# The loads of v for the first 256 queries of batch 0 go to ScalarE's queue, and the order of the beginning is ranked anew

## The chip, the core and the metric

The kernel runs on one core of one Trainium2 chip. The metric is the device time of one execution in microseconds (us); a lower time is better. One execution was also recorded by the profiler, and every time below is from that recording or from the list of executions.

## What is computed

Block-causal attention over 8 batches, 8 heads, 576 positions and head size 64 in float32, and on its output a SwiGLU feed-forward layer with 512 model columns and 1536 hidden columns.

```python
scores = scale * np.matmul(q, k.transpose(0, 1, 3, 2))
mask = block_i >= block_j                  # blocks of 64 positions
scores = np.where(mask, scores, -1000000000.0)
scores = scores - np.max(scores, axis=-1, keepdims=True)
attn = np.exp(scores)
attn = attn / (np.sum(attn, axis=-1, keepdims=True) + 1e-09)
x = np.matmul(attn, v)                     # then heads side by side: 4608 rows of 512
g = x @ w_gate
out = (g * sigmoid(g) * (x @ w_val)) @ w_out
```

## The kernel before, in words

The program is a list of tasks, each for one engine: TensorE (PE), VectorE (DVE), ScalarE (ACT), GpSimd (POOL) or SyncE's DMA queue (SP). A task has a rank, a cost, the tasks it waits for and the buffers it takes. A planner in the program (`in_order`) runs through time with these costs: whenever an engine is free, it takes the ready task with the lowest rank whose buffers are free. What comes out is the order in which each engine gets its instructions. On the chip each engine works through its own list in that order and waits where something is not there yet. So a change of ranks changes no computation, only the order on each engine, and which of several like buffers a task gets.

**Attention.** `attention(R, b, h, ...)` makes the tasks of one pair of heads. For batches 0 and 1 the pairs are cut into the first 256 queries (0 to 256) and the rest (256 to 576). `FIRST` holds a rank for each of the four pairs of each part, used for loads and values (R) and, less 0.1, for scores (Q). For 0 to 256 two pairs share one set of buffers, as two lanes. The steps and their lines:
- L411: two loads each for q and k (one per head), into `qk`. Only for the first 256 queries of batch 0 does k go through ScalarE's queue; the rest goes through SP's.
- L435 on PE: turns q and k with `ident`; L443 on ACT copies them to `parts`.
- L461 on PE: scores into PSUM. For the first 256 queries of batch 0 they stay there: L503 hides what may not be seen, L506 copies a first part to `mx`, both on ACT, and L726 and L729 on DVE take the maximum over key chunks. Otherwise L479 copies them to `sc`, L493 hides, L729 takes the maximum.
- L733 on POOL: maximum over the 128 partitions. L757 on DVE: subtracts it. L761 on ACT: Exp.
- L778: the loads of v, ranked `LATER` behind R. L801 on PE: values and, in batch 0, sums by a product with `ones`.
- L828 to L835 on DVE: invert the sums and divide; L355 and L358 split the result in a high and a low part, the x of the feed-forward tile.

**Weights.** `weight(i, kind)` brings blocks of 128 hidden columns of w_gate, w_val and w_out (kinds 0, 1, 2), in this fixed order: L968 loads 512 KB on SP; L983 and L987 on ACT and L992 and L997 on DVE build a float32 from the words; L1002 on ACT and L1005 on DVE make the high and low part. L1024 stores w_out's parts. `PIECES[i]` ranks the steps of block i, `AHEAD` the load alone.

**Feed-forward.** L1124 on PE makes gate and value products, L1223 to L1225 the output products; from tile 12 on another scheme with L1498 and L1619 to L1621. `SIDE` ranks the first two tiles among the attention.

**Later batches.** Rank `10 + b - LEAD`; their scores and maxima stand `EAGER` ahead of that. L672 are their score products.

Where the planner sees a gap for PE before 215 us, `keep_busy` puts in products of `ones` (L1836) whose result nobody reads.

Of the kernel before, what the change touches and what calls it, by code (L numbers as in the profile page):

```python
# [18 lines left out]
def kernel(  # L19
# [17 lines left out]
    nc = tc.nc  # L37
# [3 lines left out]
    P = 128  # L41
# [4 lines left out]
    SP = NKC * P  # L46
# [3 lines left out]
    XT = 256  # L50


    LEAD, EAGER = 1.69311, 0.3

    SUMS = 2
    ALONE = 3
# [4 lines left out]

    FINE = 4

    AHEAD = {(0, 1): 2.01, (0, 2): 2.07, (1, 0): 2.03, (1, 1): 2.5, (1, 2): 2.5}
    LATER = 0.6

    PIECES = [
        (2.46498, 1.85126, 2.0295),
        (4.86232, 5.94853, 3.63137),
        (4.59615, 2.52017, 1.48427),  # L70
        (3.86967, 3.05824, 5.34888),
        (1.93206, 3.59139, 2.41171),
        (5.13877, 6.90631, 5.83015),
        (3.57653, 2.93377, 2.93471),
        (0.0797053, 1.36382, 0.915695),
        (-2.09572, -5.85789, -4.34371),
        (-7.47749, -5.87222, -3.82425),
        (-7.64215, -9.14061, -8.44419),
        (-12.1092, -9.50108, -10.8836),
    ]  # L80

    SIDE = (2.97811, 4.18833)

    PATIENCE = 10.0
    FILL = 0.6

    FIRST = {
        0: [(0, 256, (-4.21445, 2.40818, 2.05548, 2.12375)), (256, 576, (-2.9124, -2.06995, -6.61901, -4.10645))],
        1: [(0, 256, (4.0214, 3.93624, 4.15916, 3.63076)), (256, 576, (-2.93177, 1.89587, 2.55533, 4.50202))],
    }  # L90
    PAIRS = 3
    PLAIN = NT // XT - 2 * PAIRS
# [62 lines left out]
    def add(engine, cost, rank, fn, after=(), bufs=(), port=False, mode=""):  # L155


        t = Task(engine, cost, rank, fn, after, bufs, port, mode)
        for a in after:
            if a is not None:  # L160
                a.next.append(t)
                t.waits += 1
        for u in bufs:
            u.left += 1
        t.n = len(tasks)
        tasks.append(t)
        return t
# [198 lines left out]
    def attention(R, b, h, a, e, early, bufs, lane):  # L366
# [10 lines left out]
        qk, prt, sc, mx, vt, xu, sr = bufs  # L377
# [393 lines left out]

        ps = Buf("at", also=banks)

        def load_v():
            nf = e // P
            for j, hd in enumerate(heads):
                cols = slice(j * D, (j + 1) * D)
                nc.sync.dma_start(  # L778
                    out=vt[0][:, 2 * lane : 2 * lane + nf, cols],
                    in_=v[b, hd, 0 : nf * P].rearrange("(c p) d -> p c d", p=P),  # L780
                )
            if e > nf * P:
# [155 lines left out]
    def weight(i, kind):  # L938
# [154 lines left out]
    def feed_forward(j, t0, w, xs):  # L1093
# [777 lines left out]
```

## Time and profile before

| what | us |
|---|---|
| median of 3 executions (1148.14 to 1149.58) | 1148.32 |
| the profiled execution, its own time | 1151.43 |
| its span, first to last instruction | 1149.7 |
| PE busy in it | 1127.7 |
| DVE, ACT, POOL busy | 888.5, 605.4, 320.9 |

An engine that is busy for 98% of the span leaves some 22 us in which it could be faster without less work; the stretches of the trace show where these lie. PE's busy time holds the products of `ones` too.

### The profile page before, as it was taken

The numbers are of one execution on the slowest core, as the hardware profiler recorded it, in microseconds if no ns is written. First come the engines' busy times: TensorE is split into PE (matmuls) and PEld (weight loads), VectorE is DVE, ScalarE is ACT, GpSimd is POOL, SyncE is SP. The second block draws the span as 40 slices with busy tenths as digits, with TensorE's granted clock in tenths as the row PEclk, the third lists the DMA queues.
The fourth block names the chain that finished last, engine by engine and source line by source line (L and its number), as shares of the span: only waits on it lengthen the run. The fifth ranks groups of instructions, "written<-read, shape, count | busy, mean of one in ns | idle before, by whom it ended". The sixth has DMA issues, their size and how long they took to land.

```text
span 1149.7 us, 22749 instructions
## 1 busy us (share of the span) xinstructions
PE 1127.7 (98%) x8728; PEld 995.9 (87%) x8728; DVE 888.5 (77%) x1526; ACT 605.4 (53%) x1126; POOL 320.9 (28%) x139
## 2 busy tenths in 40 slices
PE   7999999999999999999999999999999999999998
PEld 5677778898899898888888889888999999999997
DVE  5899898687787889989899898888753855656554
ACT  5888777565554555455565555455422433334323
POOL 3213111036643543334434535444320000000000
PEclk9999999999999999999999999999999999999999
DMA  8767757676665767876786758673468867767761
GB/s 196 192 183 186 204 167 267 171 210 182 167 158 147 203 178 206 225 220 173 206 224 186 207 159 246 175 205 119 167 235 259 272 217 235 236 229 247 234 201 69
DMA packets 294445, 228.92 MB, mean 199 GB/s; under 512 B 196608, under 2 KB 245008, under 8 KB 294336
## 3 DMA queue, kind: packets, MB, share of 16 engines
q1 hardware_dynamic: 291760, 226.75, 67.3%
q8 instruction: 68, 1.11, 0.4%
q10 hardware_dynamic: 2576, 0.72, 0.3%
q14 instruction: 41, 0.34, 0.1%
HBM read 190.45 MB, written 36.96 MB: 198 GB/s over the span
## 4 chain that ended last, share of the span: by engine, by line
PE 84%; DMA 5%; DVE 4%; ACT 4%; SPq 1%; issue 1%; POOL 0%; DVEq 0%; POOLq 0%; ACTq 0%
PE gv L1124 31%; PE gv L1498 15%; PE at L801 6%; PE at L672 6%; PE po L1223 5%; PE po L1224 5%; PE po L1225 5%; PE po L1620 1%; PE po L1619 1%; PE at L1621 1%; PE po L1621 1%; PE at L1620 1%; PE at L1619 1%; DMA wo<-in_moe_w_val_dram 1%; DMA wo<-in_moe_w_gate_dram 1%
## 5 line engine op out<-in xcount | busy, mean ns | idle before, releaser
L852 POOL PARTITION_ALL_REDUCE mx<-mx x48 | 180.1, 3799 | 212.0 <-DVE mx L729 153.8
L733 POOL PARTITION_ALL_REDUCE mx<-mx x80 | 138.3, 1778 | 309.6 <-DVE mx L729 218.9
L1124 PE MATMUL gv<-xhl,v_all 128*128 128x256 f32 x1728 | 219.3, 279 | 1.7 <-DVE v_all L1005 1.1
L1124 PEld LDWEIGHTS gv<-xhl,v_all 128*128 128x128 f32 x1728 | 206.5, 188 | 7.4 <-issue 2.8
L757 DVE TENSOR_TENSOR sc<-sc,mx 128x640 f32<-128x640 f32 (+6 forms) x168 | 123.6, 774 | 16.4 <-POOL mx L733 16.4
L761 ACT ACTIVATE sc<-sc 128x1024 f32<-128x1024 f32 (+3 forms) x104 | 106.2, 1032 | 48.0 <-DVE sc L757 47.4
L1124 PE MATMUL gv<-xhl,g_even 128*128 128x256 f32 x864 | 117.9, 281 | 0.0
L1124 PE MATMUL gv<-xhl,g_odd 128*128 128x256 f32 x864 | 116.9, 282 | 0.0
L1124 PEld LDWEIGHTS gv<-xhl,g_even 128*128 128x128 f32 x864 | 110.8, 188 | 6.9 <-issue 1.9
L729 DVE TENSOR_TENSOR mx<-mx,sc 128x128 f32<-128x128 f32 (+2 forms) x180 | 110.9, 619 | 2.1 <-ACT sc L493 0.4
L1124 PEld LDWEIGHTS gv<-xhl,g_odd 128*128 128x128 f32 x864 | 106.2, 188 | 5.1 <-issue 2.6
L1223 PE MATMUL po<-wo,hhl 128*128 128x512 f32 x252 | 101.6, 403 | 0.0
L1224 PE MATMUL po<-wo,hhl 128*128 128x512 f32 x252 | 98.7, 392 | 0.0
L1225 PE MATMUL po<-wo,hhl 128*128 128x512 f32 x252 | 98.3, 390 | 0.0
L801 PE MATMUL at<-sc,v 128*64 128x128 f32 (+4 forms) x848 | 90.0, 361 | 2.2 <-ACT parts L443 1.4
L689 ACT ACTIVATE sc<-at 128x576 f32<-128x576 f32 (+1 forms) x96 | 75.8, 835 | 27.7 <-PE at L672 27.6
L1176 ACT CAST hhl<-t 128x512 fp32r<-128x512 f32 x72 | 44.7, 621 | 82.8 <-DVE t L1171 70.8
L801 PEld LDWEIGHTS at<-sc,v 128*64 128x64 f32 x848 | 56.0, 137 | 35.8 <-ACT parts L443 1.6
L1179 DVE TENSOR_TENSOR hhl<-t,hhl 128x512 fp32r<-128x512 f32 x72 | 71.3, 990 | 17.2 <-ACT hhl L1176 17.2
L729 DVE TENSOR_TENSOR mx<-sc 128x896 f32<-128x896 f32 (+2 forms) x68 | 70.0, 1031 | 7.4 <-ACT sc L701 3.9
L672 PE MATMUL at<-parts,qk 64*128 64x288 f32 (+4 forms) x864 | 73.3, 310 | 0.7 <-ACT sc L689 0.7
L672 PEld LDWEIGHTS at<-parts,qk 64*128 64x128 f32 x864 | 62.0, 185 | 9.6 <-issue 1.1
(223 smaller groups left out, 2041.2 us busy)
## 6 DMA issues: line engine op xcount, KB each, us to landing
wo<-wo_d SPq DMA_DIRECT2D x164, 512.0 KB
v_all<-sum_d SPq DMA_DIRECT2D x36, 512.0 KB
v_all<-sum_d SPq DMA_DIRECT2D x72, 256.0 KB
sum_d<-wo SPq DMA_DIRECT2D x48, 256.0 KB
v<-in_v_dram SPq DMA_DIRECT2D x64, 128.0 KB
qk<-in_q_dram SPq DMA_DIRECT2D x112, 72.0 KB
out_dram<-ob SPq DMA_DIRECT2D x30, 256.0 KB
qk<-in_k_dram SPq DMA_DIRECT2D x104, 72.0 KB
```

Source lines behind the costliest of these rows:

```text
L672: nc.tensor.matmul(ps[0][:, x, o : o + w], lhsT=part(1, kl)[own(x), c * P : (c + 1) * P], rhs=part(0, ql)[own(x), qs : qs + w], start=n == ...
L729: nc.vector.tensor_tensor(into, prev, of(c), op)
L733: nc.gpsimd.partition_all_reduce(m, m, channels=P, reduce_op=bass_isa.ReduceOp.max)
L757: nc.vector.tensor_tensor(piece(c), scores_of(c), m, ALU.subtract)
L761: nc.scalar.activation(x, x, AF.Exp)
L801: nc.tensor.matmul(ps[0][own(x), 1 - i if sums else i, q0 - s0 : s1 - s0], lhsT=ones if sums else vt[0][:, 2 * lane + c, own(x)], rhs=sc[0 ...
L852: nc.gpsimd.partition_all_reduce(m, m, channels=P, reduce_op=bass_isa.ReduceOp.add)
L1124: nc.tensor.matmul(o, lhsT=hilo[a][:, d], rhs=xs[d][1][b][:, 0:w], start=ds[0] == 0 and n == 0, stop=ds[-1] == NDC - 1 and n == len(trio) - 1,
L1223: nc.tensor.matmul(po, lhsT=hi, rhs=whi, start=i + y == 0, stop=False)
L1224: nc.tensor.matmul(po, lhsT=hi, rhs=wlo, start=False, stop=False)
L1225: nc.tensor.matmul(po, lhsT=lo, rhs=whi, start=False, stop=i + y == NFC - 1)
L1498: nc.tensor.matmul(ps[0][:, half * XT : (half + 1) * XT], lhsT=stationary(a, j, s), rhs=part(o, j, m), start=begin and k == 0, stop=all(a ...
```

## The change

The numbers of `LEAD`, `EAGER`, `AHEAD`, `LATER`, `PIECES`, `SIDE` and `FIRST` are others (two rows of them are shown), and the loads of v for the first 256 queries of batch 0 go through ScalarE's queue.

```diff
-    LEAD, EAGER = 1.69311, 0.3
+    LEAD, EAGER = 1.571386, 3.533263
...
-    AHEAD = {(0, 1): 2.01, (0, 2): 2.07, (1, 0): 2.03, (1, 1): 2.5, (1, 2): 2.5}
+    AHEAD = {(0, 1): -0.083496, (0, 2): 1.482327, (1, 0): -5.864524, (1, 1): 2.679334, (1, 2): 8.33569}
...
-        def load_v():
+        other = early and a == b == 0
+
+        def load_v(queue=nc.scalar if other else nc.sync):
             nf = e // P
             for j, hd in enumerate(heads):
                 cols = slice(j * D, (j + 1) * D)
-                nc.sync.dma_start(
+                queue.dma_start(
                     out=vt[0][:, 2 * lane : 2 * lane + nf, cols],
                     in_=v[b, hd, 0 : nf * P].rearrange("(c p) d -> p c d", p=P),
                 )
...
-        vl = dma(R + (LATER if early else 0.0), 512.0 * e, load_v, [], [vt], 3 if e % P else 2, packet=256)
+        vl = dma(R + (LATER if early else 0.0), 512.0 * e, load_v, [], [vt], 3 if e % P else 2, "ACT" if other else "SP", 256)
```

Lines behind L771 move down by two in the changed kernel. Each engine has the same instructions as before but for the eight loads, some products of `ones` (107 instead of 96) and the PSUM buffers. TensorE's last 1866 matmuls stand in the same order; ahead of that much moves.

**SP's first issues.** `qk_0_138` and `qk_0_146` (after: `qk_0_145`) are the two buffers for q and k, `v_0_78` and `v_0_80` the two for v, `wo_0_...` the five for weights. Before:

```order
L411 DMA qk_0_138<-in_q_dram 96x3x64 x2
L778 DMA v_0_78<-in_v_dram 128x2x64 x2
L411 DMA qk_0_146<-in_q_dram 96x3x64 x4
L411 DMA qk_0_138<-in_q_dram 96x3x64 x2
L968 DMA wo_0_108<-in_moe_w_gate_dram 128x4x256
L778 DMA v_0_80<-in_v_dram 128x2x64 x4
L778 DMA v_0_78<-in_v_dram 128x2x64 x2
L411 DMA qk_0_138<-in_q_dram 96x4x64 x2
L411 DMA qk_0_138<-in_k_dram 96x6x64 x2
L968 DMA wo_0_109<-in_moe_w_val_dram 128x4x256
```

After:

```order
L411 DMA qk_0_138<-in_q_dram 96x3x64 x2
L411 DMA qk_0_145<-in_q_dram 96x3x64 x2
L411 DMA qk_0_138<-in_q_dram 96x3x64 x2
L411 DMA qk_0_145<-in_q_dram 96x3x64 x2
L970 DMA wo_0_108<-in_moe_w_gate_dram 128x4x256
L411 DMA qk_0_138<-in_q_dram 96x4x64 x2
L411 DMA qk_0_138<-in_k_dram 96x6x64 x2
L970 DMA wo_0_109<-in_moe_w_val_dram 128x4x256
```

The eight issues of v are gone, and the second lane of `qk_0_138` comes ahead of that of the other buffer.

**ScalarE's start.** Before:

```order
L411 DMA qk_0_138<-in_k_dram 96x3x64 x2
L1664 ACT_TABLE_LOAD
L1664 ACTIVATE seen<-seen 128x1
L411 DMA qk_0_146<-in_k_dram 96x3x64 x4
L411 DMA qk_0_138<-in_k_dram 96x3x64 x2
L443 ACTIVATE parts_0_86<-gv_0_169 128x288
L443 ACTIVATE parts_1_87<-gv_0_175 128x288
L503 ACTIVATE at_0_155<-at_0_155,unseen 128x4x64
L506 COPY mx_0_201<-at_0_155 128x2x128
```

After, from the fourth row on (ahead of it stand two issues each of k for `qk_0_138`, v for `v_0_78` and k for `qk_0_145`):

```order
L411 DMA qk_0_138<-in_k_dram 96x3x64 x2
L1666 ACT_TABLE_LOAD
L1666 ACTIVATE seen<-seen 128x1
L443 ACTIVATE parts_0_86<-gv_0_170 128x288
L443 ACTIVATE parts_1_87<-gv_0_176 128x288
L411 DMA qk_0_145<-in_k_dram 96x3x64 x2
L780 DMA v_0_80<-in_v_dram 128x2x64 x2
L503 ACTIVATE at_0_156<-at_0_156,unseen 128x4x64
L443 ACTIVATE parts_0_86<-gv_0_170 128x288
L443 ACTIVATE parts_1_87<-gv_0_176 128x288
L780 DMA v_0_78<-in_v_dram 128x2x64 x2
L506 COPY mx_0_228<-at_0_156 128x2x128
```

All eight first issues stand ahead of the table load now, and six issues and two copies stand between the first operands (L443) and L506. The last two issues of v follow after four more rows. Further down, the conversion of the first w_gate block (L1002) moved from just ahead of the first step of the first w_val block (L983) to just behind it.

**SP up to the third w_val block** (`wo_0_110`), from the stores of w_out's first parts on. Before (the q and k of `qk_0_138` that stand second after the change stand ahead of these rows):

```order
L1024 DMA wo_d<-g_even_75 128x4x128
L1024 DMA wo_d<-g_even_77 128x4x128
L411 DMA qk_0_146<-in_q_dram 96x3x64 x2
L411 DMA qk_0_146<-in_k_dram 96x3x64 x2
L778 DMA v_0_80<-in_v_dram 128x4x64 x2
L783 DMA v_0_80<-in_v_dram 64x2x64
L411 DMA qk_0_146<-in_q_dram 96x3x64 x2
L411 DMA qk_0_146<-in_k_dram 96x3x64 x2
L968 DMA wo_0_109<-in_moe_w_gate_dram 128x4x256
L411 DMA qk_0_138<-in_q_dram 96x3x64 x2
L968 DMA wo_0_110<-in_moe_w_val_dram 128x4x256
```

After:

```order
L1026 DMA wo_d<-g_even_75 128x4x128
L1026 DMA wo_d<-g_even_77 128x4x128
L411 DMA qk_0_138<-in_q_dram 96x4x64 x2
L411 DMA qk_0_138<-in_k_dram 96x6x64 x2
L411 DMA qk_0_145<-in_q_dram 96x3x64 x2
L411 DMA qk_0_145<-in_k_dram 96x3x64 x2
L780 DMA v_0_80<-in_v_dram 128x4x64 x2
L785 DMA v_0_80<-in_v_dram 64x2x64
L970 DMA wo_0_108<-in_moe_w_gate_dram 128x4x256
L411 DMA qk_0_145<-in_q_dram 96x3x64 x2
L411 DMA qk_0_145<-in_k_dram 96x3x64 x2
L970 DMA wo_0_110<-in_moe_w_val_dram 128x4x256
```

The stores stand first, the third w_gate block stands ahead of the last q and k of `qk_0_145`, and the q pair ahead of w_val is gone from there.

## Rows read from the trace of the kernel before

**Rows 1.** The page: the span and TensorE's busy time.

```profile
span 1149.7 us, 22749 instructions
PE 1127.7 (98%) x8728; PEld 995.9 (87%) x8728; DVE 888.5 (77%) x1526; ACT 605.4 (53%) x1126; POOL 320.9 (28%) x139
```

**Rows 2.** Load by stretch: from and to in us, length, then busy time and instructions of each engine, TensorE's granted clock as a share of full speed, share of the DMA engines, GB/s.

```profile
0.00:41.04 41.04, 32.20 (x323) 26.03 (x324) 27.24 (x69) 27.06 (x53) 14.12 (x20) 0.96 0.77 194
10.00:15.00 5.00, 3.53 (x36) 2.94 (x36) 2.77 (x6) 3.79 (x10) 1.51 (x2) 1.00 0.72 174
15.00:20.00 5.00, 4.44 (x54) 3.91 (x54) 3.33 (x9) 2.07 (x6) 4.20 (x4) 1.00 1.02 239
...
75.00:215.00 140.00, 135.59 (x1005) 110.79 (x1004) 122.93 (x212) 107.21 (x194) 23.37 (x19) 1.00 0.69 201
100.00:120.00 20.00, 19.96 (x158) 16.30 (x155) 17.10 (x30) 15.75 (x32) 5.82 (x4) 1.00 0.93 224
600.00:800.00 200.00, 200.00 (x1600) 177.83 (x1598) 176.88 (x282) 106.74 (x188) 92.75 (x32) 1.00 0.67 190
```

**Rows 3.** TensorE up to 75 us: its longest wait (total, times, longest), and the busy time of L1836 alone in that stretch.

```profile
PE at L461 <- ACT parts L443: 4.1, 3, 3.1
...
0.00:75.00 75.00, 16.48 (x192) 14.05 (x192) 0.98 0.72 184
```

**Rows 4.** SP's queue in order of time: start, length, line, what is issued, how many.

```profile
0.73 0.91 SPq L411 DMA_DIRECT2D qk<-in_q_dram  x2
...
3.17 4.03 SPq L411 DMA_DIRECT2D qk<-in_q_dram  x6
...
7.84 2.99 SPq L778 DMA_DIRECT2D v<-in_v_dram  x6
10.93 1.58 SPq L411 DMA_DIRECT2D qk<-in_q_dram  x2
...
14.61 0.51 SPq L968 DMA_DIRECT2D wo<-in_moe_w_val_dram  x1
...
34.31 0.85 SPq L411 DMA_DIRECT2D qk<-in_q_dram  x2
...
45.08 0.47 SPq L968 DMA_DIRECT2D wo<-in_moe_w_gate_dram  x1
...
46.65 0.47 SPq L968 DMA_DIRECT2D wo<-in_moe_w_val_dram  x1
```

**Rows 5.** ScalarE in order of time (ACTq: its DMA issues; in brackets the idle time before the row and what ended it).

```profile
0.74 0.96 ACTq L411 DMA_DIRECT2D qk<-in_k_dram  x2
1.73 1.28 ACT L1664 ACT_TABLE_LOAD   x1 [1.73 <-PEq L1854]
...
3.47 2.42 ACTq L411 DMA_DIRECT2D qk<-in_k_dram  x4
5.93 0.71 ACT L443 ACTIVATE parts<-gv 128x288 f32<-128x288 f32 x2 [2.71 <-DMA qk<-in_k_dram]
7.67 0.45 ACT L503 ACTIVATE at<-at,unseen 128x256 f32<-128x256 f32 x1 [1.02 <-PE at L461]
8.15 0.37 ACT L506 COPY mx<-at 128x256 f32<-128x256 f32 x1
...
20.40 0.78 ACT L983 ACTIVATE ob<-wo 128x512 f16<-128x512 f32 x1 [3.33 <-DMA wo<-in_moe_w_val_dram]
...
22.52 0.63 ACT L443 ACTIVATE parts<-at 128x576 f32<-128x576 f32 x1
...
52.46 0.79 ACT L983 ACTIVATE ob<-wo 128x512 f16<-128x512 f32 x1 [1.20 <-DMA wo<-in_moe_w_val_dram]
```

**Rows 6.** VectorE's waits up to 41.04 us: total, times, longest.

```profile
DVE sc L757 <- POOL mx L733: 3.5, 2, 2.2
DVE wo L992 <- ACT ob L983: 1.8, 2, 1.3
DVE sr L828 <- PE at L801: 1.2, 1, 1.2
```

**Rows 7.** VectorE in order of time.

```profile
8.55 0.42 DVE L726 COPY mx<-at 128x256 f32<-128x256 f32 x1 [4.17 <-ACT mx L506]
...
41.04 2.93 DVE L757 TENSOR_TENSOR sc<-sc,mx 128x640 f32<-128x640 f32 x5
...
53.44 0.45 DVE L828 STREAM_TRANSPOSE sr<-po 128x256 f32<-128x256 f32 x1 [1.25 <-ACT sr L895]
```

**Rows 8.** TensorE in order of time, between 306 and 318 us: products of 128 rows (L1124) and a block of products of 64 rows (L672).

```profile
306.82 0.51 PE L1124 MATMUL gv<-xhl,g_even 128*128 128x256 f32 x3
307.26 1.07 PE L672 MATMUL at<-parts,qk 64*128 64x288 f32 x12
...
315.96 1.57 PE L1124 MATMUL gv<-xhl,g_even 128*128 128x256 f32 x12
317.37 0.87 PE L1124 MATMUL gv<-xhl,g_odd 128*128 128x256 f32 x6
```

**Rows 9.** The chain that ended last, its first two pieces: start, length, what; a load's length runs from issue to landing.

```profile
0.74 2.71 DMA qk<-in_k_dram
3.47 2.90 DMA qk<-in_k_dram
```

More of the change, by code (lines that the diff above doesn't have):

```diff
@@ L62 @@
     FINE = 4
-    AHEAD = {(0, 1): 2.01, (0, 2): 2.07, (1, 0): 2.03, (1, 1): 2.5, (1, 2): 2.5}
-    LATER = 0.6
+    AHEAD = {(0, 1): -0.083496, (0, 2): 1.482327, (1, 0): -5.864524, (1, 1): 2.679334, (1, 2): 8.33569}
+    LATER = 0.595047
     PIECES = [
[L68 to L79, printed above, removed]
+        (2.46498, 1.85126, 1.989959),
+        (3.078149, 5.94853, 4.5426),
+        (5.243281, -1.760877, -0.59026),
+        (3.314534, 5.058387, 7.706737),
+        (2.073692, 6.770616, 1.885983),
+        (-1.674509, 7.596873, 5.770771),
+        (8.760551, 3.105905, 9.704257),
+        (0.045307, 1.36382, 0.244583),
+        (-1.025389, -0.885477, -4.516175),
+        (-7.289443, -6.137035, -6.344597),
+        (-7.64215, -9.202601, -6.57203),
+        (-20.296957, -11.697245, -12.264919),
     ]
-    SIDE = (2.97811, 4.18833)
+    SIDE = (2.97811, 4.689617)
     PATIENCE = 10.0
@@ L87 @@
     FIRST = {
-        0: [(0, 256, (-4.21445, 2.40818, 2.05548, 2.12375)), (256, 576, (-2.9124, -2.06995, -6.61901, -4.10645))],
-        1: [(0, 256, (4.0214, 3.93624, 4.15916, 3.63076)), (256, 576, (-2.93177, 1.89587, 2.55533, 4.50202))],
+        0: [(0, 256, (-7.882981, 2.009396, 1.545746, 2.12375)), (256, 576, (-3.938665, -3.824963, -14.529285, -4.103347))],
+        1: [(0, 256, (3.274971, 5.869312, 2.105466, 3.587042)), (256, 576, (-2.910293, 1.091971, 2.928513, 8.395196))],
     }
@@ L782, in load_v @@
             if e > nf * P:
-                nc.sync.dma_start(
+                queue.dma_start(
                     out=vt[0][0 : e - nf * P, nf, :].rearrange("p (h d) -> p h d", h=2),
```

## The prediction

> **What bounds the kernel now.** I read the page first, then TensorE's load by stage, its waits, and then the first 55 us engine by engine, since the change works there. The page shows TensorE busy for 1127.7 of 1149.7 us [rows 1]. By stage it is full between 600 and 800 us (200.00 of 200), and between 75 and 215 us it lacks 4.4 of 140 us [rows 2]. So from some 75 us on the time is TensorE's own work, and a change pays only by what TensorE idles, or fills with products of `ones` that nobody reads, before that. Those fillers take 16.48 us, all before 75 us, and the waits come on top: 4.1 us for score operands that ScalarE evicts (3.1 of them in one piece) [rows 3]. Before 75 us TensorE is starved, and the engines to ask are ScalarE, VectorE and the loads.
>
> The long piece of 3.1 us is read on ScalarE: it stood idle 3.33 us until the first w_val block landed, converted it at 20.40, and only behind that, at 22.52, evicted the operands [rows 5]. ScalarE works in order, so an eviction that was ready waited behind a weight. That load was issued at 14.61 [rows 4], 5.8 us before. And SP reached it late: it ran from 0.73 to 10.83 through q and v issues, and took up the next q loads at 10.93 [rows 4].
>
> **Part 1, eight loads of v leave SP's queue.** Six of them took 2.99 us [rows 4], 0.50 each, so SP gains 4.0 us. The whole cannot be had: the next q and k loads overwrite a buffer whose transposes need the loads of the second head pair. These are now SP's third pair instead of its fifth, so they can be issued by about 4 us instead of 7; the last k pair of ScalarE (below: issued by 5.9, landing 2.7 to 2.9 later [rows 9]) then lets the transposes run at some 8.4 to 9.0. I put the next q loads at 9.1 instead of 10.93 and, with the shorter row of issues, w_val at 12.0 instead of 14.61: 2.6 us earlier. Both ends: 10.6 by issue time alone, 14.6 if nothing comes of it. It lands at 17.8 if it takes as long as before.
>
> Against this speaks the load of the DMA engines: their share is 1.02 between 15 and 20 us [rows 2], so a load issued earlier need not land earlier. From 10 to 15 us it was 0.72, so there is room for what moves forward into that stretch, and I take most of the 2.6 us. The Trainium skill, "DMA: Bandwidth & Descriptors", section "Issuing engines are not separate DMA queues", holds that loads issued by several engines share the same 16 DMA engines and that a second issuing queue saves only issue time. By that rule alone the gain would be SP's 4.0 us of issue at the most and, at a share of 1.02, nothing; the rows leave a part, because SP's issue was what the w_val load waited for.
>
> **Part 2, the same eight issues land on ScalarE.** Two queues show the same habit: four loads issued back to back, the fifth only when the first has landed. ScalarE's fifth is issued at 3.47, the first landed at 3.45 [rows 5, 9]. Before, ScalarE issued eight k loads until 5.89, with the table load in between at 1.73 [rows 5]. After, eight issues (k, v, k, k in pairs) stand ahead of the table load. They end at the same 5.9, then the table load (1.28) and the small Exp (some 0.2) follow: the first operands are evicted at 7.4, not 5.93, so 1.5 later. Then four issues (0.48 each by 0.96 for two, 1.9 together) stand ahead of the masking copy of L503; 1.0 of them lies under the wait for the scores that was there anyway (6.64 to 7.67), 0.9 adds. Then two evictions (0.71) and two issues (0.96) stand ahead of L506: 1.7. So L506, which VectorE waits for, comes 4.1 us later, at 12.2 instead of 8.15 [rows 5], and VectorE's first maximum at 12.6 instead of 8.55 [rows 7]. This is a loss, and its cover is only that later waits of VectorE shrink.
>
> From L506 on ScalarE has eleven operations of 0.37 to 0.78 us and one pair of issues, 6.8 us, until w_val's conversion: 19.0 instead of 20.40. The load is there by then (17.8), so its wait goes. One conversion of the first w_gate block (some 0.7; its neighbour of the same width took 0.78) now stands behind instead of ahead, so the eviction of the operands comes at 21.8 instead of 22.52.
>
> **Part 3, the sum for VectorE.** From 30 us on VectorE is what all wait for, and it has the same amount of work ahead of the subtraction that starts at 41.04 [rows 7]: one weight step more of one kind, one less of another, of one length. Until then it worked 27.24 us [rows 2] and idled 13.8. After: the first wait is 4.1 longer. Of the other 9.6, with 3.5 for maxima from GpSimd, 1.8 for ScalarE's part of the weights and 1.2 for value products in them [rows 6], I expect 4.1 to stay: weight steps now fill the waits for GpSimd, w_val no longer stalls, the second value products come 1.6 us earlier. So 4.2 + 4.1 + 4.1 = 12.4 idle: the row is reached **1.4 us earlier**. Ends: 4.1 later if nothing shrinks, 2.6 earlier if the w_val load sets all.
>
> **Part 4, the third w_val block.** SP issued it at 46.65, behind a buffer wait that ended at 34.31 and a row of q, k and v issues [rows 4]. ScalarE idled 1.20 us for it until 52.46, and VectorE 1.25 until 53.44 behind ScalarE [rows 5, 7]. After, one pair of q issues (0.9 us, as SP's first pair) no longer stands ahead of it and the row begins some 1 us earlier: issued near 44.7, landed near 50.5. The wait shrinks to about 0.4: **0.8 us**. Ends 0 and 1.25.
>
> **Part 5, ranks behind the beginning.** LEAD and EAGER set when later batches' scores are issued. TensorE is full there, so only its own work counts: a turn between products of 64 rows and of 128. Three products take 0.44 us ahead of such a turn (306.82 to 307.26) and 0.35 in a run of twelve (1.41 from 315.96 to 317.37) [rows 8]: 0.09 a turn, and I take the same on the way back, so 0.2 a block. Counted over TensorE's whole order, blocks of scores and value products fall from 120 to 116, two of the four in the beginning where it costs nothing: I take 0.6 of 0.4 to 0.8 us: **0.6 us**.
>
> **Sum.** 1.4 + 0.8 + 0.6 = 2.8. Of the 2.2 us of head start I give 0.4 back between 100 and 120 us, where the DMA share is 0.93 [rows 2] and weights that are wanted earlier cannot come earlier. That leaves 2.4 us: from this execution's span 1149.7 to 1147.3, its own time from 1151.4 to 1149.0, and since that execution stood 3.1 above the median, the median of 1148.3 goes to **1145.9 us**. A measurement of this kernel can tell about 0.2% (2.3 us) from no change, so the forecast stands right at that line.
>
> **Rivals.**
> *The loads land no earlier* (DMA engines full). For it: 1.02 in 15 to 20 us. Against it: 0.72 just before. Then w_val is converted at 20.4 again, the 1.4 goes, and part 4's 0.8 halves: 0.4 + 0.6, some 1.0 us, **1147.3**. Chance 0.27.
> *ScalarE is held by its own queue* (the other sign). Its 13th to 16th loads of v fall behind four that are under way. When a landing takes 5.8 us, as w_val's did, and not the 2.7 of the first [rows 9], each of these pairs holds ScalarE some 2.5 to 3 us more, with the first exponentials behind it. It decides if landings exceed about 4 us before 16 us. Price 5.2 us on the sum: **1151.1**. For it: share 1.02 from 15 us. Against it: these issues come before that. Chance 0.18.
> *The head start grows.* From 75 to 215 us the missing 4.4 us [rows 2] are waits on weights; w_gate and w_val blocks stand some ten rows earlier on SP's queue there. If half of it goes as well, **1143.5**. Chance 0.15.
> *The forecast* itself: 0.40, its own range 1144.3 to 1147.4.
>
> **Numbers.** 1142.5 to 1150.0 leaves out the upper half of the second rival and the far end of the third. Faster by over 0.2% is below 1146.0: a little over half of the forecast (0.22), all of the third (0.15) and a corner of the first (0.05), 0.42. Slower is above 1150.6: 0.14. The rest, 0.44, is the same.
>
> **What would show it.** Right: ScalarE's L506 near 12 us; w_val issued near 12 and converted near 19 with no wait; the five subtractions of 41.04 near 39.6; the third w_val issued near 44.7; TensorE's last filler earlier, by some 2 us. Wrong: a wait on ScalarE ahead of its v issues at 11 to 16 us, w_val still landing past 20, or VectorE's first maximum past 13 with the subtractions not before 41; or new waits of TensorE between 75 and 215 us, which no term here holds.

## The result, and the profile after

The changed kernel takes **1159.18 us** (median of 5 executions, 1155.72 to 1161.64) against 1149.09 for the kernel before: 1.008 times its time, 95% interval 1.0064 to 1.0097. The forecast was 1145.9 us in a range to 1150.0, so it was wrong in sign and size. The profiled execution took 1159.42 us.

The page of the changed kernel, its span and the busy time of each engine (us, share, instructions):

```profile
span 1157.6 us, 22793 instructions
PE 1132.7 (98%) x8750; PEld 1000.1 (86%) x8750; DVE 893.7 (77%) x1526; ACT 602.3 (52%) x1126; POOL 324.0 (28%) x139
```

Against [rows 1] TensorE is busy some 5 us more (1.8 of them in products of `ones`) and idle some 3 us more. Neither tells where. First the places that the prediction named. Timelines of the changed kernel on ScalarE (first five rows; ACTq: its DMA issues), VectorE (two) and SP (four); columns: start, duration in us, engine, line (two lines lower down than before from L778 on), operation, and in brackets the idle time ahead and what ended it:

```profile
11.14 1.13 ACTq L780 DMA_DIRECT2D v<-in_v_dram  x2
12.31 0.37 ACT L506 COPY mx<-at 128x256 f32<-128x256 f32 x1 [0.77 <-DMA wo<-in_moe_w_gate_dram]
19.56 0.79 ACT L985 ACTIVATE ob<-wo 128x512 f16<-128x512 f32 x1 [0.48 <-DMA wo<-in_moe_w_val_dram]
22.07 0.63 ACT L443 ACTIVATE parts<-at 128x576 f32<-128x576 f32 x1
24.94 0.77 ACT L985 ACTIVATE ob<-wo 128x512 f16<-128x512 f32 x1 [2.24 <-DMA wo<-in_moe_w_out_dram]
...
12.71 0.42 DVE L726 COPY mx<-at 128x256 f32<-128x256 f32 x1 [8.33 <-ACT mx L506]
40.57 2.92 DVE L757 TENSOR_TENSOR sc<-sc,mx 128x640 f32<-128x640 f32 x5
...
10.65 0.84 SPq L411 DMA_DIRECT2D qk<-in_q_dram  x2
11.82 0.86 SPq L411 DMA_DIRECT2D qk<-in_k_dram  x2
12.73 0.50 SPq L970 DMA_DIRECT2D wo<-in_moe_w_val_dram  x1
43.70 0.47 SPq L970 DMA_DIRECT2D wo<-in_moe_w_val_dram  x1
```

L506 came at 12.31 (forecast 12.2), VectorE's first maximum at 12.71 (12.6), the w_val load at 12.73 (12.0) and its conversion at 19.56 (19.0), the third w_val load at 43.70 (44.7). The five subtractions came at 40.57 instead of 39.6; before they stood at 41.04 [rows 7]. So up to there the rows came near the places that were worked out for them, though not always for the reasons given (see the part on the prediction). What followed did not. One sign of being wrong that the prediction named did show: between 75 and 215 us TensorE was busy for 134.34 us instead of 135.59 [rows 2], with a wait of 2.2 us for a weight step of VectorE in it. SP's queue after 52 us:

```profile
52.94 0.61 SPq L922 DMA_DIRECT2D s_d<-sr  x1
60.57 0.38 SPq L970 DMA_DIRECT2D wo<-in_moe_w_gate_dram  x1
```

and the load by stretch (busy us and instructions of PE, PEld, DVE, ACT, POOL; then TensorE's granted clock, DMA share, GB/s):

```profile
50.00:55.00 5.00, 5.00 (x46) 4.09 (x43) 4.06 (x9) 4.56 (x10) 3.37 (x2) 1.00 0.72 195
55.00:60.00 5.00, 3.48 (x26) 2.52 (x25) 5.00 (x10) 5.00 (x11) 0.00 (x0) 1.00 0.01 3
...
480.00:490.00 10.00, 7.64 (x66) 6.68 (x64) 8.86 (x10) 3.75 (x9) 9.81 (x4) 0.98 0.68 157
490.00:500.00 10.00, 10.00 (x76) 9.70 (x77) 9.63 (x19) 8.80 (x16) 0.00 (x0) 0.85 0.46 142
```

For 7 us SP stood at a w_gate load and the DMA engines were empty (0.01). And at 480 to 500 us, where the prediction had TensorE full, it was idle for 2.4 us and then had 0.85 of its clock. That second place, engine by engine (GpSimd, VectorE, ScalarE, TensorE):

```profile
478.56 4.09 POOL L733 PARTITION_ALL_REDUCE mx<-mx  x2 [18.82 <-issue]
482.56 7.26 POOL L854 PARTITION_ALL_REDUCE mx<-mx  x2
...
482.04 0.75 DVE L654 TENSOR_TENSOR qk<-sr,qk 128x576 fp32r<-128x576 f32 x1
482.70 3.01 DVE L1181 TENSOR_TENSOR hhl<-t,hhl 128x512 fp32r<-128x512 f32 x1
486.04 0.28 DVE L1287 TENSOR_TENSOR wo<-wo 128x128 f32<-128x128 f32 x1
486.36 2.54 DVE L1288 TENSOR_TENSOR wo<-wo 128x128 f32<-128x128 f32 x1
...
488.93 0.62 ACT L1294 CAST wo<-wo 128x512 fp32r<-128x512 f32 x1 [4.39 <-DVE wo L1288]
489.45 0.36 ACT L701 ACTIVATE sc<-at,unseen 128x128 f32<-128x128 f32 x1
...
482.16 1.47 PE L672 MATMUL at<-parts,qk 64*128 64x288 f32 x12
485.06 1.52 PE L1126 MATMUL gv<-xhl,v_all 128*128 128x256 f32 x12
486.51 1.13 PE L672 MATMUL at<-parts,qk 64*128 64x448 f32 x12
489.87 1.75 PE L672 MATMUL at<-parts,qk 64*128 64x320 f32 x12 [2.22 <-ACT sc L701]
491.55 2.36 PE L1126 MATMUL gv<-xhl,v_all 128*128 128x256 f32 x12
```

Read from below: TensorE's second score product (486.51 and 489.87) waits 2.22 us in its middle for ScalarE's masking copy L701, which empties its PSUM buffer; L701 stands in order behind a weight eviction (L1294) that waits 4.39 us for VectorE; and VectorE's last of four short sums took 2.54 us instead of 0.28, beside two pairs of GpSimd reductions without a gap. Behind the wait come the other half of the score product, at 1.75 us, and twelve gate products that take 2.36 us instead of 1.52.

**A ledger.** To find where time goes between two traces, I added up TensorE's useful products in the order of each trace (fillers left out), each at the duration that such a product has when nothing holds it, and read when the same sum is reached. The table gives the lag behind the trace of before at five points (us of that trace); the last column is the lag gained from 460 to 777 us, where most of the later batches lie. Runs with the same order differ by up to 3.7 us in the first 261 us, so single entries there say little; and pricing a product by its mean spacing in the trace of before instead moves entries by up to 2 us and the last column by up to 1.1.

| run | median us | ratio to before, 95% | 86 | 261 | 460 | 777 | 1036 | 460 to 777 |
|---|---|---|---|---|---|---|---|---|
| changed kernel | 1159.2 | 1.0064 to 1.0097 | 2.9 | 2.9 | 3.1 | 7.9 | 8.9 | 4.8 |
| e1 | 1155.2 | 1.0035 to 1.0062 | 1.8 | -1.6 | -1.3 | -1.7 | 5.1 | -0.3 |
| e2 | 1150.3 | 0.9994 to 1.0018 | -2.2 | -3.7 | -3.4 | -2.0 | -1.3 | 1.4 |
| e3 | 1183.2 | 1.0276 to 1.0318 | 1.8 | 6.0 | 7.9 | 15.9 | 32.6 | 8.1 |
| e4 | 1167.7 | 1.0140 to 1.0179 | -0.3 | 7.5 | 9.4 | 12.6 | 14.0 | 3.2 |
| f1 | 1152.0 | 1.0016 to 1.0048 | 0.3 | -1.0 | 0.2 | 0.7 | 0.8 | 0.5 |
| f2 | 1158.9 | 1.0072 to 1.0106 | 2.6 | -0.3 | -0.6 | 6.2 | 7.3 | 6.8 |
| f3 | 1152.8 | 1.0017 to 1.0054 | 2.6 | 1.2 | 0.9 | 2.7 | 2.9 | 1.9 |
| f4 | 1156.6 | 1.0053 to 1.0084 | 4.6 | 1.4 | 1.9 | 6.9 | 7.9 | 5.1 |
| h1 | 1151.4 | 1.0007 to 1.0029 | 2.5 | 1.5 | 2.3 | 2.9 | 3.2 | 0.6 |
| h2 | 1154.7 | 1.0035 to 1.0078 | -1.3 | -5.1 | -4.9 | 2.1 | 2.9 | 7.0 |
| h4 | 1159.3 | 1.0060 to 1.0110 | -0.8 | -1.6 | -0.9 | 8.8 | 9.7 | 9.6 |
| h5 | 1158.5 | 1.0041 to 1.0094 | 0.9 | -0.6 | -0.5 | 6.6 | 7.9 | 7.1 |
| h6 | 1151.0 | 1.0000 to 1.0026 | -1.1 | -2.4 | -2.3 | 0.0 | 0.7 | 2.2 |
| h7 | 1158.5 | 1.0060 to 1.0101 | 0.5 | -3.7 | -3.6 | 7.5 | 7.7 | 11.0 |
| k1 | 1152.3 | 1.0018 to 1.0048 | 1.8 | -1.7 | -2.9 | -1.3 | 1.8 | 1.6 |
| k2 | 1154.8 | 1.0036 to 1.0069 | 0.4 | -4.1 | -3.7 | 3.1 | 3.6 | 6.7 |
| k3 | 1153.1 | 1.0019 to 1.0042 | 2.6 | 0.3 | 0.6 | 1.0 | 4.9 | 0.4 |
| k4 | 1159.2 | 1.0066 to 1.0104 | 2.3 | -1.0 | -0.4 | 11.9 | 12.3 | 12.3 |

The medians of before beside these runs lay between 1148.7 and 1150.0 us.

### The profile page after: what moved, and what is told of

Read it like the earlier page. It is cut to its first block, busy times and chain, and to the rows that moved or that the text cites. A ratio compares the mean times of both kernels' runs of the same rounds, so it can differ in the third digit from the quotient of the medians.

```text
span 1157.6 us, 22793 instructions
## 1 busy us (share of the span) xinstructions
PE 1132.7 (98%) x8750; PEld 1000.1 (86%) x8750; DVE 893.7 (77%) x1526; ACT 602.3 (52%) x1126; POOL 324.0 (28%) x139
## 3 DMA queue, kind: packets, MB, share of 16 engines
q10 hardware_dynamic: 4752, 1.25, 0.5%
q8 instruction: 69, 1.13, 0.4%
## 4 chain that ended last, share of the span: by engine, by line
PE 78%; DVE 9%; DMA 8%; ACT 3%; issue 1%; SPq 1%; POOL 0%; ACTq 0%; DVEq 0%
PE gv L1126 28%; PE gv L1500 15%; PE at L803 6%; PE at L672 5%; PE po L1225 5%; PE po L1226 4%; PE po L1227 4%; DMA wo<-in_moe_w_out_dram 2%; DVE sc L757 2%; PE po L1621 1%; DMA xt<-x_d 1%; PE po L1622 1%; PE po L1623 1%; DMA qk<-in_k_dram 1%; PE at L1623 1%; PE at L1622 1%
## 5 line engine op out<-in xcount | busy, mean ns | idle before, releaser
L733 POOL PARTITION_ALL_REDUCE mx<-mx x80 | 141.9, 1823 | 388.0 <-DVE mx L729 231.3
L1126 PE MATMUL gv<-xhl,v_all 128*128 128x256 f32 x1728 | 222.6, 280 | 2.6 <-DVE v_all L1007 2.2
L854 POOL PARTITION_ALL_REDUCE mx<-mx x48 | 180.7, 3809 | 133.7 <-DVE mx L729 72.0
L729 DVE TENSOR_TENSOR mx<-mx,sc 128x128 f32<-128x128 f32 (+2 forms) x180 | 104.6, 596 | 0.7
L803 PE MATMUL at<-sc,v 128*64 128x320 f32 (+4 forms) x896 | 95.1, 361 | 0.3
L803 PEld LDWEIGHTS at<-sc,v 128*64 128x64 f32 x896 | 59.5, 137 | 35.4 <-issue 0.7
L672 PE MATMUL at<-parts,qk 64*128 64x288 f32 (+4 forms) x864 | 74.5, 312 | 2.4 <-ACT sc L701 2.2
L1181 DVE TENSOR_TENSOR hhl<-t,hhl 128x512 fp32r<-128x512 f32 x72 | 67.5, 938 | 11.0 <-ACT hhl L1178 10.9
L1173 DVE SCALAR_TENSOR_TENSOR t<-t,gv 128x512 f32<-128x512 f32 x72 | 49.1, 682 | 32.0 <-PE gv L1126 31.2
L672 PEld LDWEIGHTS at<-parts,qk 64*128 64x128 f32 x864 | 62.8, 187 | 12.0 <-issue 2.5
```

The costliest lines, as they stand in the source:

```text
L672: nc.tensor.matmul(ps[0][:, x, o : o + w], lhsT=part(1, kl)[own(x), c * P : (c + 1) * P], rhs=part(0, ql)[own(x), qs : qs + w], start=n == ...
L729: nc.vector.tensor_tensor(into, prev, of(c), op)
L733: nc.gpsimd.partition_all_reduce(m, m, channels=P, reduce_op=bass_isa.ReduceOp.max)
L803: nc.tensor.matmul(ps[0][own(x), 1 - i if sums else i, q0 - s0 : s1 - s0], lhsT=ones if sums else vt[0][:, 2 * lane + c, own(x)], rhs=sc[0 ...
L854: nc.gpsimd.partition_all_reduce(m, m, channels=P, reduce_op=bass_isa.ReduceOp.add)
L1126: nc.tensor.matmul(o, lhsT=hilo[a][:, d], rhs=xs[d][1][b][:, 0:w], start=ds[0] == 0 and n == 0, stop=ds[-1] == NDC - 1 and n == len(trio) - 1,
```

## Experiments: one part at a time (e1 to e4)

Two theories at the start: the new beginning costs (its ranks, or ScalarE's queue), or the order that the planner lays out behind it does. The edits, against the changed kernel (e1, e4) and against the kernel before (e2, e3):

```diff
-    LEAD, EAGER = 1.571386, 3.533263
+    LEAD, EAGER = 1.69311, 0.3
...
-    LEAD, EAGER = 1.69311, 0.3
+    LEAD, EAGER = 1.571386, 3.533263
...
-                nc.sync.dma_start(
+                queue.dma_start(
...
-        other = early and a == b == 0
+        other = False
```

**e1**, LEAD and EAGER as before. Expected: 

> The changed kernel with LEAD and EAGER of before; TensorE's first 2653 matmuls keep the changed order, so the beginning is that of the changed kernel. Theory 1 (two separate losses: some 2.5 us are lost before 260 us by the new beginning, some 5.5 us later by the scores that LEAD and EAGER move, 4 of these in one stall near 490 us): the stall near 490 us goes, the beginning's loss stays: 1151.5 to 1153. Theory 2 (the beginning is the whole cause, and what comes later follows from its being late): stays at 1156 to 1160. Theory 3 (any order that was not tried out loses a few us somewhere): anything between, with a new stall at a new place.

**e2**, only those two as changed. Expected: 

> The kernel of before with LEAD and EAGER of the change; TensorE's first 2944 matmuls keep the order of before. Theory 1: some 5 us slower than before, 1153 to 1156, with the loss behind 300 us. Theory 2: as before, 1148 to 1150. Theory 3: 1150 to 1156, with a stall of TensorE behind a ScalarE or VectorE step that GpSimd's reductions slow down, not at 490 us.

**e3**, only v on ScalarE's queue. Expected: 

> The kernel of before with the eight loads of v on ScalarE's queue and all ranks of before. Theory 1 says nothing of this by itself: if the queue is what costs in the beginning, some 2.5 us slower up to 260 us. By my ledger of the first 55 us (the first maximum 4 us later, regained by 40 us) the queue itself costs nothing by 55 us. Theory 3: 1151 to 1158, since the ranks were not made for it.

**e4**, all new ranks, v on SP. Expected: 

> The changed kernel with the eight loads of v back on SP's queue, all new ranks kept. Theory 1: the late loss stays (LEAD and EAGER are new), so 1153 to 1160; if the queue is what costs in the beginning, the 2.5 us up to 260 us go. Theory 3: 1152 to 1160 with stalls at other places than in the changed kernel.

Measured: 1155.15, 1150.26, 1183.18 and 1167.67 us. e1 and e2 fell in the range of theory 3 alone, e3 and e4 above every range given. Nothing adds up: half of the change costs more than the whole, and two numbers that cost nothing on the old beginning (e2) cost 3.6 us on the new one (the ratio of the changed kernel less that of e1). Each half leaves the planner in a state of its own, and all that comes behind is laid out anew. e4 is 7.5 us behind at 261 us already; what holds it there was not followed up. Where e3 and e1 lost most shows in the waits of TensorE in e3 (from 440 to 900 us; total, times, longest) and in its stretch in e1:

```profile
PE gv L1500 <- ACT xhl L1387: 11.4, 1, 11.4
PE po L1225 <- DMA wo<-wo_d: 3.7, 2, 3.5
```

```profile
865.00:870.00 5.00, 2.24 (x11) 1.54 (x9) 4.28 (x10) 2.98 (x8) 0.00 (x0) 1.00 0.81 279
870.00:875.00 5.00, 4.78 (x25) 4.41 (x26) 2.24 (x7) 0.95 (x3) 0.00 (x0) 0.72 0.97 349
```

The 11.4 us of e3 and the stretch of e1 (2.76 us idle at 869.93, for the same step) are the hand-over from the tiles of 512 to the pairs of tiles, whose x was not converted in time: 800 us behind the edit. e3's second row is a late load of w_out's parts, 3.46 us of it at 497.9. So a total time cannot judge the beginning; the beginning and the later order had to be crossed.

## Experiments: beginning and later order crossed (f1 to f4)

The planner gets the other kernel's list of tasks (`PLAN`) and, from FROM = 60 us of its own time, lets each engine take only the next task of that list. Below it, f4's edit on the changed kernel:

```diff
+                if now >= FROM:
...
+                    cand = [t for t in left_of[e][:1] if t in cand]
...
+    order.insert(at[3082], order.pop(at[3057]))
```

**f1.** Expected: 

> The changed kernel, but from 60 us of the planner's time on each engine takes its tasks in exactly the order in which the kernel before has them (the new beginning with the old rest). Theory 'later order': the beginning is worth what the first 55 us showed, 1 to 2.4 us, and all of the loss comes from the order laid out behind it, so 1147.0 us (1145 to 1149), with no wait of TensorE near 490 us. Rival 'the beginning itself': what SP, ScalarE and VectorE do before 60 us leaves weights or buffers late, and the debt is paid later in whatever order, so 1155 to 1159 us.

**f2.** Expected: 

> The crossed case: the kernel before up to 60 us of the planner's time, and from there exactly the changed kernel's order on each engine. Theory 'later order': the loss comes along, 1158 to 1161 us, with the wait near 490 us in the trace. Rival 'the beginning itself': about as before, 1149 us (1147 to 1151).

**f3.** Expected: 

> The v loads on ScalarE's queue alone, all ranks as before, and from 60 us on exactly the order of the kernel before (with its own later order this edit took 1183.2 us). Theory 'later order': the 34 us were all in the order, so 1146 to 1151 us. Rival 'the beginning itself': the queue without the new ranks starts worse and stays so, 1153 us or more; its trace showed TensorE 4.3 us behind by 145 us, so 1153.5 us if that is the beginning's.

**f4.** Expected: 

> The changed kernel with one task of ScalarE's order moved: the eviction of a mixed weight block near 489 us (high of mix, which waited 4.39 us for VectorE) is issued behind the masking copy and the tanh that stood behind it, and nothing else. Theory 'later order': the 2.22 us wait of TensorE and the stretch at 0.85 of its clock go, some 4 us: 1155.2 us (1154 to 1157). Rival 'the beginning itself': TensorE's debt shows at the next place, 1158 to 1160 us.

f2 settles the first question: the beginning of before with the changed kernel's later order takes 1158.87 us, as slow as the changed kernel. f3 shows the reverse: all but some 4 of the 34 us of e3 were the order, since with the old rest it takes 1152.82 us. But f1 took 1151.97, between the two ranges given for it: the new beginning is no gain either, it costs 0.32% (0.16 to 0.48). In f1's trace 480 to 500 us is whole, and the score operand is ready 7 us ahead of its product there (VectorE, then TensorE):

```profile
485.02 0.75 DVE L654 TENSOR_TENSOR qk<-sr,qk 128x576 fp32r<-128x576 f32 x1
...
492.71 1.06 PE L672 MATMUL at<-parts,qk 64*128 64x288 f32 x12
```

In the changed kernel it ended at 482.79 (482.04 + 0.75), 0.6 after the product had begun. f4 removed the 2.22 us wait as meant, and took 1156.59 us, in the first range, but its interval (1.0053 to 1.0084) overlaps that of the changed kernel; its trace has instead a wait of 1.60 us for that operand at 483.20, so the stall moved one step up the chain.

## Experiments: the late weight step, and where the later order loses (h1, h2, h4 to h7)

In the changed kernel VectorE makes the low part of a g_odd block only at 59.85 (the kernel before: at 49.03, 19 of VectorE's instructions earlier in its order); the w_gate load of 60.57 needs its buffer. h1 (on f1) and h2 (on the changed kernel) move that one task; h4, h5 and h6 move the switch; h7 gives TensorE alone another list.

```diff
+    order.insert(at[117], order.pop(at[1649]))
...
+    FROM = 500.0
...
+                        cand = [t for t in cand if t.n == TENSOR[len([u for u in order if u.engine == e])]]
```

**h1.** Expected: 

> The new beginning with the old rest (1152.0 us), and in it one task of VectorE moved: the low part of a g_odd block, which stood 13 tasks behind the place where its high part is ready and for which SP's next w_gate load waited 6.8 us (53 to 60 us), now stands ahead of them. Theory 'late weight step': the load is issued by 54 us, the DMA share of 0.01 in 55 to 60 us goes, TensorE is not behind at 61 us, and the 3.2 us that the beginning costs go: 1148.9 us (1147 to 1150.5); if the head start of the forecast was there beneath, 1146.5 us. Rival 'SP is not what TensorE waits for': the load comes earlier and the time stays, 1151 to 1153 us.

**h2.** Expected: 

> The changed kernel with the same one task of VectorE moved and nothing else. Theory 'late weight step': the beginning's share goes and that of the later order stays, 1156 us (1154 to 1157.5). Rival 'SP is not what TensorE waits for' (the changed kernel's trace had this debt back by 168 us): 1158 to 1160 us.

**h4.** Expected: 

> The kernel before up to 500 us of the planner's time (some 520 us on the chip), and from there the changed kernel's order on each engine. Taken from 60 us on, that order cost 10.1 us. Theory 'one stretch': 6 of them are lost between 420 and 505 us, where two pairs of GpSimd reductions stand back to back, and 1 at the hand-over to the pair tiles near 860 us, so 1151 us (1149.5 to 1152.5) with this switch. Rival 'spread': the new order is worse all along, so about half stays, 1153.5 to 1156 us.

h2 took 1154.67 us, in the range of the theory, and h1 1151.43, in that of the rival. In h2 SP issues the load at 53.43, and the DMA engines work (SP's timeline, then the load by stretch):

```profile
53.43 0.38 SPq L970 DMA_DIRECT2D wo<-in_moe_w_gate_dram  x1
```

```profile
55.00:60.00 5.00, 3.16 (x27) 2.20 (x26) 4.90 (x11) 5.00 (x11) 0.00 (x0) 1.00 0.67 198
```

TensorE did not get busier in that stretch (3.16 of 5 against 3.48), but at 261 us h2 is 5.1 us ahead in the ledger where the changed kernel was 2.9 behind. Both pairs moved the same way, by 2.8 us (changed kernel to h2) and 1.6 (f1 to h1) in their ratios to before; their intervals overlap, so the task is a likely part of the loss, not a shown one, and its size is open.

h4 (1159.32 us, above both ranges) refuted "one stretch": the whole loss stayed, now at 510 to 520 us. The last set asked why.

**h5.** Expected: 

> The kernel before up to 600 us of the planner's time, from there the changed kernel's order. The run with the switch at 500 lost 8 us at 510 to 520 us, where it takes the next two products of scores 12.7 us of TensorE's work earlier than the kernel before; the changed kernel takes those ahead of them 12.9 and 14.2 us earlier and loses at 480 to 500 us. Behind 600 us it takes no score products more than 4.4 us earlier. Theory 'scores too early': nothing is lost but the 1 us at the hand-over, 1150 us (1148.5 to 1151.5). Rival 'spread' (any stretch of the new order is worse): 1153 us or more.

**h6.** Expected: 

> The changed kernel with the g_odd task of VectorE moved, in its own order up to 400 us of the planner's time, and then in the order of the kernel before. Its trace without the old rest was 5 us ahead of the kernel before at 440 us, and lost it from there. Theory 'scores too early': the lead stays, 1147.5 us (1145.5 to 1149.5). Rival 'spread': the new order had cost its share by 400 us, 1151 to 1154 us.

**h7.** Expected: 

> The changed kernel with the g_odd task of VectorE moved (1154.7 us by itself), and TensorE's order changed in one more place: the two score products of 482 to 490 us stand where the kernel before has them, 12.9 and 14.2 us of TensorE's work later; the other engines follow (46 tasks of VectorE by up to 21 places, GpSimd's two back-to-back pairs stay). Theory 'scores too early': the wait of 2.2 us and the low clock at 480 to 500 us go, 4 to 5 us, 1150.2 us (1149 to 1152). Rival 'GpSimd alone' (the two pairs of reductions stall whatever stands there): 1153.5 to 1156 us.

h5 (1158.54) and h7 (1158.47) refuted "scores too early" as I had put it. In h7 the two score products were gone from the place of the stall, and TensorE stalled there all the same, now at gate and value products that wait for VectorE (VectorE, then TensorE):

```profile
480.13 2.54 DVE L1288 TENSOR_TENSOR wo<-wo 128x128 f32<-128x128 f32 x1
482.59 0.67 DVE L1168 SCALAR_TENSOR_TENSOR t<-t,gv 128x512 f32<-128x512 f32 x1
...
483.31 1.68 PE L1126 MATMUL gv<-xhl,g_even 128*128 128x256 f32 x12 [3.10 <-DVE t L1168]
487.90 2.99 PE L1126 MATMUL gv<-xhl,v_all 128*128 128x256 f32 x24 [1.55 <-DVE t L1173]
```

The four reductions stand ahead of it as in the changed kernel (472.33 to 483.58), and the same short sum takes 2.54 us. So at this place it is VectorE that is behind, and a score product is only one of the things that wait for it: what happened is what the rival "GpSimd alone" says, though at 1158.47 us its range was missed too. The same four reductions do not stall TensorE in e1, with EAGER 0.3 (GpSimd, then the load by stretch):

```profile
480.80 4.08 POOL L733 PARTITION_ALL_REDUCE mx<-mx  x2 [16.72 <-ACT t L1165]
484.79 7.25 POOL L854 PARTITION_ALL_REDUCE mx<-mx  x2
...
480.00:490.00 10.00, 10.00 (x79) 9.51 (x77) 8.94 (x11) 2.40 (x5) 9.20 (x4) 1.00 0.68 196
```

By these three traces neither the reductions nor the score products alone make the stall; it takes VectorE slowed beside GpSimd and an order that leaves TensorE nothing in hand. In h5 the losses are a wait of 2.0 us at 631 us, again for VectorE's L1166, and one of 2.5 at the scores of 661.

h6 (1150.96) says that the new order up to 400 us of the planner's time costs little or nothing (0 to 3 us). h7 shows how thin it is further on. Its VectorE and TensorE, and below the same tasks of f2, which have the same order there:

```profile
653.12 0.43 DVE L1280 TENSOR_TENSOR wo<-g_even,g_even 128x256 f32<-128x256 f32 x1 [2.29 <-DMA sum_d<-wo]
...
661.03 0.80 PE L672 MATMUL at<-parts,qk 64*128 64x288 f32 x8 [2.29 <-DVE qk L654]
```

```profile
653.46 0.43 DVE L1278 TENSOR_TENSOR wo<-g_even,g_even 128x256 f32<-128x256 f32 x1
...
660.90 1.27 PE L672 MATMUL at<-parts,qk 64*128 64x288 f32 x12
```

TensorE came to this block 2.7 us earlier in h7, but VectorE's buffer was freed by a store at the same time, and the lead went as a wait of 2.29 us. f2 was just late enough not to wait.

## Experiments: LEAD and EAGER apart (k1 to k4)

For all these traces it was counted, of the 14 or 15 score blocks between 370 and 760 us, in how many the operand (the end of L654's qk) is ready less than 0.3 us ahead of the first product L672. I call such a block tight. In the changed kernel and f2, f4, h2 with its order: 4, 4, 5 and 4; in e4 5; in h4, h5 and h7, which have parts of it, 3, 2 and 2; in before, e1, f1, h1 and h6: none. The two kinds differ in EAGER, by which a score product's rank stands ahead of its batch: at 3.53 it goes ahead of the gate and value products as soon as the planner thinks its operand ready. Four kernels hold the beginning (with the g_odd task moved) and the hand-over (the order of before from 780 us) alike:

```diff
-    LEAD, EAGER = 1.571386, 3.533263
+    LEAD, EAGER = 1.571386, 0.3
...
+    FROM = 780.0
```

**k1.** Expected: 

> Beginning of the changed kernel with the g_odd task moved, EAGER 0.3 as before and LEAD 1.571386 as changed; from 780 us of the planner's time the order of the kernel before, so that the hand-over to the pair tiles is the same in all four of this set. Theory 'no slack': EAGER is what sets each score product right behind its operand (in the changed kernel's order the operand is ready 1.2 us ahead in the median, in that of before 2.5), so with 0.3 the median slack is 2 us or more, no stall stands between 440 and 700 us, 1148 us (1146 to 1150). Rival 'LEAD': 1152 us or more. Rival 'any untried order': 1150 to 1156 us without a pattern over the four.

**k2.** Expected: 

> The same with both numbers as changed (LEAD 1.571386, EAGER 3.533263). All theories: the changed kernel with the g_odd task moved, 1154.7 us, less the 1 us of its hand-over, 1153.7 us (1152 to 1156), and 5 us lost between 440 and 700 us. It is the mark that the other three are read against.

**k3.** Expected: 

> The same with both numbers as before (LEAD 1.69311, EAGER 0.3). With the task where it was and its own hand-over this was 1155.2 us, of which its trace lost 6.5 us at the hand-over alone. Theories 'no slack' and 'LEAD': 1147.5 us (1145.5 to 1149.5). Rival 'any untried order': 1150 to 1156 us.

**k4.** Expected: 

> The same with LEAD as before and EAGER as changed. Theory 'no slack': as with both new, 1153 us (1151 to 1156), median slack near 1 us. Rival 'LEAD': as with both old, 1147 to 1149.5 us. Rival 'any untried order': anywhere in 1150 to 1156 us.

| | EAGER 0.3 | EAGER 3.533263 |
|---|---|---|
| LEAD 1.571386 | k1: 1152.28 us, lost 1.6 from 460 to 777, tight blocks 0 | k2: 1154.79 us, lost 6.7, tight 4 |
| LEAD 1.69311 | k3: 1153.07 us, lost 0.4, tight 0 | k4: 1159.17 us, lost 12.3, tight 2 |

TensorE's waits between 440 and 700 us in k1, k2 and k4 (k3 has none):

```profile
PE at L672 <- ACT sc L689: 1.0, 2, 0.5
```

```profile
PE at L672 <- ACT sc L701: 2.2, 1, 2.2
PE at L672 <- DVE qk L654: 1.8, 2, 1.3
```

```profile
PE at L672 <- DVE qk L654: 4.0, 2, 2.8
PE gv L1126 <- DVE t L1168: 2.7, 1, 2.7
PE gv L1126 <- DVE t L1173: 0.9, 1, 0.9
```

In that stretch of the traces EAGER costs 5 us at the new LEAD and 12 at the old one; LEAD alone, at EAGER 0.3, costs 1. In the times it is clear only at the old LEAD (k4 against k3); the intervals of k1 and k2 overlap. k1 and k3 missed the expected 1148 and 1147.5 us, mainly because they lost 3.1 and 3.9 us more behind 777 us, at the switch at 780 us, where k2 and k4 lost 0.5 and 0.4. k4 lies above every range given, and the sign that the theory named for it failed: its operands were ready 2.6 us ahead in the median, not 1. Of its waits 4.0 us are for score operands, and 3.6 are gate and value products that wait for VectorE, as in h7.

Other traces do not fit. e2 has EAGER 3.53 and four tight blocks and lost only 1.4 us; f3 and e3 have 0.3 and still two and three tight blocks, and e3 lost 8.1 us, 3.46 of them at the late load of w_out's parts. And the count does not rank the losses: k4 lost most, with two tight blocks. So TensorE waits for VectorE, or for ScalarE behind it; EAGER makes that likely, and how much it costs hangs on the rest of the order. What spares e2 stays open, and that EAGER acts through tight blocks is argued, not shown.

No version beat the kernel before: h6 (1.0000 to 1.0026) and e2 (0.9994 to 1.0018) come nearest.

## Why the prediction was wrong

**Part 1, right in sign, in part by luck.** The w_val load went out 1.9 us earlier (12.73 against 14.61 [rows 4]), but not by the step that was to bring it: the next q loads went out at 10.65 and not at 9.1, only 0.3 earlier than before, because SP waited 3.5 us for the transposes, which TensorE ran at 9.88, behind the first scores, and not at 8.4 to 9.0. What was gained is that the row from there to w_val took 2.1 us instead of 3.7 (2.9 in the forecast), above all because the pair of k loads in it took 0.86 us; before it was

```profile
12.60 1.96 SPq L411 DMA_DIRECT2D qk<-in_k_dram  x2
```

The conversion of w_val came only 0.8 earlier (19.56 against 20.40 [rows 5]). The rest went to a longer way: 6.8 us from issue to conversion, 5.8 before. The DMA share was 0.85 from 10 to 15 us and 1.11 from 15 to 20, against 0.72 and 1.02 [rows 2]. The Trainium skill, "DMA: Bandwidth & Descriptors", section "Issuing engines are not separate DMA queues", says that loads from several engines share one set of DMA engines; with these shares the trace agrees.

**Part 2, right.** L506 and the first maximum came within 0.1 us of the forecast. The idle time of 0.77 us ahead of L506 is the two v issues that were put there (11.14 to 12.27, 1.13 us instead of 0.96); the second of them waited until the w_gate load had landed at 11.81. The rival "ScalarE is held by its own queue" fell: no pair of v issues held it 2.5 us. Its sign was right, its reason was not.

**Part 3, too large, and the rest luck.** 0.5 us instead of 1.4. VectorE idled 14.3 us up to the row, not 12.4: the first wait grew by 4.2 as forecast, but the others shrank to 6.0 us and not to 4.1. A wait of ScalarE for w_out (2.24 us at 24.94), which the sum did not hold, cost 0.8 of it. The 0.5 us came from VectorE being busy 1.0 us less up to there (26.27 against 27.24 [rows 2]), which no term held either.

**Part 4, right, in size half**: issue at 43.70, and the wait at w_val's conversion was gone; but VectorE still waited 0.83 us for ScalarE at 52.03, instead of 1.25 [rows 7].

**What bounds the kernel, and part 5: the steps that failed.** "From some 75 us on the time is TensorE's own work" was true of the one order in the trace and was used as if it held for any. Part 5 then priced LEAD and EAGER by turns between products alone (-0.6 us) and put waits of TensorE at nothing; the changed kernel lost 4.8 us between 460 and 777 us by such waits and the low clock behind them, and EAGER costs 5 to 12 us in that stretch of k1 to k4. [rows 2] has TensorE full, but no row was asked how long before each product its operand was ready; in the trace of before that is 3.8 us in the median of those 15 blocks, in the changed kernel 0.8. The changed trace was not there to ask, but how far the score products move forward could have been read from the two orders.

**Between 55 and 75 us** no term held SP's 7 us. VectorE's task further back and SP's w_gate load ahead of the store of g_odd were to be seen in the order.

**The mark itself.** The execution read for the prediction stood some 2 us above its median, and e2, whose first 250 us have the same order, was 3.7 us ahead of it at 261 us. Some of the waits that the sum meant to remove were of that one execution: TensorE's wait for evicted score operands, 4.1 us with 3.1 in one piece [rows 3], is in e2

```profile
PE at L461 <- ACT parts L443: 2.2, 3, 1.3
```

The range ended at 1150.0 because its only slow case was worked out from the first 16 us. The likeliest account of the 9.2 us (7.4 to 11.1 by the interval): some 2 to 4 from the beginning (f1, and h1 with the one task moved), 5 to 7 from 460 to 777 us (the table; f2), 1 at the hand-over. The two kernels f1 and f2 together overshoot (3.7 and 10.2 of 1149 us by their ratios), so the parts do not simply add.

## What to carry to other kernels

In a program whose order a planner makes, a change of ranks is a change of every later instruction; price it by crossing the beginning and the rest, not by the part that was edited. Where several engines are near full, ask of each product on the bounding engine how long its operand, and the buffer that it writes, have been ready: a share of busy time does not show where a shifted order can make it wait. How much it then loses was not to be had from that spare time alone (e2, k4). And a wait on the bounding engine costs more than its length when the clock falls behind it.

## What the runs showed of the hardware

- VectorE beside two GpSimd reductions without a gap: sums of 0.28 and 0.69 us took 2.54 and 3.01. The Trainium skill, "SBUF — State Buffer", section "SBUF: two separate sides", has the two engines share a port pair that one holds for its whole instruction. The trace agrees only in part: sums of 0.28 us ran between 485.64 and 486.32, in the last 0.6 us of the first of the two reductions (482.56 to 486.24; the spans on GpSimd are rough), and in the traces of before, the changed kernel and k3 the sums that were not stretched lie in the last 40% of such a reduction. Nor are such pairs the cause by themselves: the changed kernel has 14 stretches of over 9 us of reductions without a gap between 150 and 830 us, and only that at 479 us goes with a wait of TensorE of over 0.2 us; e1 has the same pairs at 480.80, and TensorE full.
- Behind a wait of 2.22 us the granted clock was 0.50 (the lower of its two levels, 1.2 GHz) from 490 to 493 us, 0.85 over the 10 us. Half a score product took 1.75 us there, where its other half and it take 1.96 together at full clock (before, 497.80), and the next twelve gate products 2.36 instead of 1.52: the wait cost some 1.7 us more than it lasted. Not every wait does: behind the 3.10 us of h7 the clock stayed at 1.00 (480 to 500 us).
- before, e2, h4 and h5 have one order up to 261 us, and their traces stand there 0, 3.7, 1.6 and 0.6 us ahead of before's: more between two of them than the whole forecast gain.
